# Maxout products of three chunks by Strassen's seven products, all v loads and nearly all stores on SyncE, and a new order table

## The chip, the cores and the metric

The kernel runs on one core of a Trainium2 chip. The metric is the device time of one execution in microseconds (us). The core has five engines that run their own instruction lists and wait for each other through semaphores: TensorE (PE; its weight loads are counted apart as PEld), VectorE (DVE), ScalarE (ACT), GpSimd (POOL) and SyncE (SP, which here only issues DMAs). Matrix products land in PSUM, which has eight banks per partition, each as wide as 512 f32 numbers; DVE or ACT must copy a result out before its bank is free for another product.

## The reference: what is computed

An attention with feature maps (8 batches, 8 heads, 576 tokens, head size 64, 128 features) feeds a maxout layer (4608 tokens, model size 512, inner size 768):

```
def phi(x):
    proj = np.einsum('bhsd,df->bhsf', x, w_phi)
    proj = proj - np.max(np.abs(proj), axis=-1, keepdims=True)
    return np.concatenate([np.exp(proj), np.exp(-proj)], axis=-1)
q_p, k_p = (phi(q), phi(k))
kv = np.einsum('bhsf,bhsd->bhfd', k_p, v)
z = np.sum(k_p, axis=2)
num = np.einsum('bhsf,bhfd->bhsd', q_p, kv)
den = np.einsum('bhsf,bhf->bhs', q_p, z)[..., None] + 1e-06
...
h = np.maximum(np.maximum(x @ w1, x @ w2), x @ w3)
return (h @ w_out).astype(np.float32)
```

Here `x` is the attention's output, with the heads side by side.

## The kernel before

**Attention** is done in 16 units: one batch and four of its eight heads each. A unit loads q and k as bf16 (POOL's DMA queue), v as f32 (`v_raw`, L435), and the last 64 tokens of q (`tail_raw`, L426). It turns q and k so that the head size lies along the partitions (`qkT`): the first four units on PE (L459), the others by transposing DMAs on SP (L478). It projects (`psk`, `psq`, `pst`, L496), takes the largest absolute value of each row on DVE (L500), and exponentials on ACT (`Ek` L504, `Eq` L584). POOL scales v by a factor per token (`vab`, L548), PE multiplies this with `Ek` (`kvps`, L567) and `Eq` with that (`psn`, L632); DVE adds the two halves (L641, L644) and POOL divides (`x_sb`, L690). A transposing DMA on SP (L722; PE in the first two units) puts the result, turned, into `xT`.

Most of the projections and the `kvps` products use 64 of PE's 128 rows at a time (`mode=1` in the code), two of them side by side. The projection of the last tokens (L600) uses all 128 rows, with a weight tile whose upper half is zero (`wph_low`).

**The maxout layer** is done in nine chunks of 512 tokens: chunks 0 to 7 are the first 512 tokens of each batch, chunk 8 is the last 64 tokens of all batches. It uses max(a, b, c) = a + max(0, b − a, c − a): POOL first replaces w2 and w3 by their differences to w1 (L844, six pieces), and since the `a` part goes through `w_out` unchanged, w1 and `w_out` are multiplied once ahead (`pm`, L865) and applied to x directly (`straight`, L781). So a chunk is 2 × 6 products `ups` (L748), each of four 128x512 matmuls; the first kind is copied out with a relu (ACT L762 or DVE L764), the second is maximized into it by DVE (L758) to give `hT`; then four groups of `straight` (four matmuls each, L781) and `down` (six, L786), a copy `osb` (L796) and a store (L800).

**The order** is no loop order: every piece of work is a node, and the table `PLAN` lists all nodes with the engine that runs them, the start for which they were set, and the buffer or PSUM bank that they take. Each engine runs its nodes in the table's order; the starts themselves have no effect on the chip, but for `fill`, which puts idle matmuls (`idler`, L911) into gaps of the first 30 us.

## Time and profile before

| | |
|---|---|
| time, median of 3 runs | 282.42 us (282.17 to 282.78) |
| span of the profiled execution, first to last instruction | 280.8 us |
| own time of the profiled execution | not listed; the median lies 1.6 us above its span |
| PE busy | 268.3 us, 3409 matmuls in the records |
| DVE busy | 217.3 us |
| ACT busy | 199.1 us |
| POOL busy | 161.5 us |
| TensorE clock granted | 1.00 throughout |

A busy share is the time in which an engine has at least one instruction under way. Matmuls overlap: one of 512 columns lasts 379 ns, but the next one starts well before it ends, so the pace of PE is read from the time that a run of equal matmuls takes, not from the mean of one. DVE and ACT instructions overlap a little in the same way.

### The profile page before, as it was taken

The page shows a single profiled execution, that of the slowest core. Times are in us where ns is not written, and L with a number is a line of the kernel's source. Part 1 is how long each engine was busy: PE and PEld are TensorE (multiplying, and loading weights), DVE is VectorE, ACT ScalarE, POOL GpSimd, SP SyncE. Part 2 cuts the span into 40 slices and gives each one's busy share as a digit, 9 for nine tenths or more (in the row PEclk, how much of TensorE's full clock was granted, in tenths as well). Part 3 has the DMA queues.
Part 4 walks back from the last instruction along what each step waited for, and adds up shares of the span by engine and source line. Part 5 has one row for each costly group of instructions (what it writes and reads, how often), then busy time and mean ns, then how long its engine had stood idle before and what let it go on. Part 6 is the DMA issues. An engine that isn't in the chain of part 4 may idle for free. (4 is left out here: it accounts for less than half of the span.)

```text
span 280.8 us, 8401 instructions
## 1 busy us (share of the span) xinstructions
PE 268.3 (96%) x3409; PEld 150.8 (54%) x3447; DVE 217.3 (77%) x442; ACT 199.1 (71%) x489; POOL 161.5 (58%) x161
## 2 busy tenths in 40 slices
PE   8789899999999999999999999999999999999993
PEld 5457654576655555555555456655546544444441
DVE  2799989999999969889997899898876871157320
ACT  4799999999999787698978879989589200310001
POOL 4879999998949703897336848393495341000000
PEclk9999999999999999999999999999999999999999
DMA  7999999997999999999999997717130224110253
GB/s 136 300 202 208 207 173 310 260 164 132 171 186 249 236 196 281 169 171 144 189 263 204 188 276 125 151 55 170 39 86 3 77 47 121 40 75 0 82 144 112
DMA packets 76214, 44.52 MB, mean 159 GB/s; under 512 B 52688, under 2 KB 67344, under 8 KB 76176
## 3 DMA queue, kind: packets, MB, share of 16 engines
q1 hardware_dynamic: 59536, 29.21, 49.8%
q0 software_dynamic: 14912, 11.77, 28.7%
q10 hardware_dynamic: 1728, 3.02, 3.0%
q8 instruction: 27, 0.44, 0.7%
q14 instruction: 11, 0.09, 0.1%
HBM read 34.64 MB, written 9.44 MB: 157 GB/s over the span
## 5 line engine op out<-in xcount | busy, mean ns | idle before, releaser
L748 PE MATMUL ups<-xT,w_bf 128*128 128x512 bf16 x414 | 101.3, 379 | 1.0
L584 ACT ACTIVATE Eq<-psm 128x512 bf16<-128x512 f32 (+1 forms) x160 | 81.7, 587 | 5.4 <-PE psm L593 3.1
L548 POOL TENSOR_TENSOR vab<-v_raw,em 128x1152 bf16<-128x1152 f32 (+1 forms) x36 | 68.2, 1907 | 22.9 <-ACT em L542 15.0
L504 ACT ACTIVATE Ek<-psk 128x512 bf16<-128x512 f32 x128 | 72.1, 633 | 8.2 <-PE psk L496 6.3
L748 PEld LDWEIGHTS <-w_bf 128*128 128x128 bf16 x432 | 39.2, 98 | 43.9 <-issue 2.3
L690 POOL TENSOR_TENSOR x_sb<-y,rden 128x640 bf16<-128x640 f32 x32 | 39.9, 1256 | 39.5 <-DVE rden L689 39.0
L786 PE MATMUL ops<-wout_bf,hT 128*128 128x512 bf16 (+2 forms) x214 | 50.5, 373 | 0.3
L758 DVE TENSOR_TENSOR hT<-hT,ups 128x512 bf16<-128x512 bf16 x54 | 35.5, 677 | 13.3 <-PE ups L748 11.1
L500 DVE TENSOR_REDUCE mq<-psq 128x4 f32<-128x512 f32 x64 | 41.2, 682 | 3.5 <-PE psq L496 3.2
L500 DVE TENSOR_REDUCE mk<-psk 128x4 f32<-128x512 f32 x64 | 41.9, 679 | 2.1 <-PE psk L496 1.7
L762 ACT ACTIVATE hT<-ups 128x512 bf16<-128x512 f32 x36 | 21.9, 620 | 24.5 <-PE ups L748 24.4
L641 DVE TENSOR_TENSOR y<-psn,sq 128x325 f32<-128x325 f32 x64 | 30.4, 491 | 6.7 <-PE psn L632 4.3
L796 ACT COPY osb<-ops 128x512 f32<-128x512 f32 x20 | 12.2, 608 | 32.3 <-PE ops L786 31.8
L786 PEld LDWEIGHTS <-hT 128*128 128x128 bf16 x222 | 20.6, 98 | 22.5 <-issue 0.2
L632 PEld LDWEIGHTS <-Eq 128*128 128x128 bf16 x640 | 26.3, 98 | 10.3 <-issue 0.4
L644 DVE TENSOR_TENSOR y<-y,psn 128x325 f32<-128x325 f32 x64 | 29.7, 487 | 1.6
L632 PE MATMUL psn<-kv_sb,Eq 128*128 128x65 bf16 x640 | 28.8, 194 | 0.2
L496 PEld LDWEIGHTS <-qkT 64*128 64x128 bf16 x576 | 18.0, 94 | 13.4 <-issue 8.3
L781 PE MATMUL ops<-xT 128*128 128x512 bf16 x87 | 23.7, 380 | 0.5
L567 PE MATMUL kvps<-vab,Ek 64*128 64x65 bf16 x1152 | 22.1, 191 | 0.8 <-POOL vab L548 0.6
L567 PEld LDWEIGHTS <-Ek 64*128 64x128 bf16 x1152 | 20.3, 94 | 3.4 <-issue 1.3
L796 DVE COPY osb<-ops 128x512 f32<-128x512 f32 (+2 forms) x17 | 11.1, 657 | 12.5 <-PE ops L786 12.5
(65 smaller groups left out, 263.9 us busy)
## 6 DMA issues: line engine op xcount, KB each, us to landing
v_raw<-in_v_dram SPq DMA_DIRECT2D x15, 576.0 KB, 6.0
out_dram<-osb SPq DMA_DIRECT2D x23, 256.0 KB, 3.3
qk_bf<-in_k_dram POOLq DMA_DIRECT2D x15, 288.0 KB, 6.9
qk_bf<-in_q_dram POOLq DMA_DIRECT2D x15, 256.0 KB, 8.7
w_bf<-in_moe_w_dram POOLq DMA_DIRECT2D x3, 768.0 KB, 13.2
out_dram<-osb ACTq DMA_DIRECT2D x9, 256.0 KB, 3.4
tail_raw<-in_q_dram SPq DMA_DIRECT2D x16, 64.0 KB, 4.8
wout_bf<-in_moe_w_out_dram POOLq DMA_DIRECT2D x1, 768.0 KB, 19.2
```

Of the source, the lines that this page charges most:

```text
L500: return nd(kind, {"DVE": 0.598 if n == 4 else 0.331}, lambda: nc.vector.tensor_reduce(dst(m()), ps()[:, 0:n, :], AXX, ALU.max, apply_abso ...
L504: return nd("ek", {"ACT": 0.478 if n == 4 else 0.264}, lambda: nc.scalar.activation(dst(Ek[g]()), ps()[:, 0:n, :], EXP, scale=1.0 - 2.0 * ...
L548: made.append(chosen(n_, lambda n_, g=g, t0=t0, t1=t1: (nc.vector if n_.eng == "DVE" else nc.gpsimd).tensor_tensor(vab()[:, g, t0:t1, 0:D] ...
L567: nc.tensor.matmul(kvps[ab]()[:, pr, g, :], lhsT=Ek[g]()[r, t, :], rhs=vab()[r, g, t, :], start=(pr == prs[0] and g + j == 0), stop=(pr == ...
L584: return nd("eq", {"ACT": 0.478 if n == 4 else 0.264}, lambda: nc.scalar.activation(Eq[g]()[:, t0:t0 + n, :], ps()[:, 0:n, :], EXP, scale= ...
L632: nc.tensor.matmul(psn[g]()[:, i, :], lhsT=Eq[g]()[:, t, :], rhs=kv()[:, pr, ab, g, :], start=True, stop=True)
L641: n_ = nd("xu", {"DVE": 0.064 + 0.0676 * n_t}, lambda: nc.vector.tensor_tensor(yv(y()), ps(0), sq_of(sq()).unsqueeze(len(shape) - 1).to_br ...
L644: return nd("xw", {"DVE": 0.064 + 0.0674 * n_t}, lambda: nc.vector.tensor_tensor(yv(y()), yv(y()), ps(1), ALU.add), [n_], [psn[1], y], loc ...
L690: divs[pr] = nd("x", {"POOL": 1.2}, lambda pr=pr, y=y, rden=rden: nc.gpsimd.tensor_tensor(x_sb()[:, pr].rearrange("p t a d -> p a t d"), y ...
L748: nc.tensor.matmul(ups()[:, o * n:(o + 1) * n], lhsT=w_bf[i + (not plain)][:, ct, jj * P:(jj + 1) * P], rhs=tokens_of(ct)[:, cols] if halv ...
L758: nc.vector.tensor_tensor(dst, dst, src, ALU.max)
L786: nc.tensor.matmul(ops_()[:, 0:hi - lo], lhsT=hT()[:, j, tt * P:(tt + 1) * P], rhs=wout_bf[:, j, lo:hi], start=plain and j == 0, stop=(j = ...
```

## The change

**Seven products.** In chunks 6, 7 and 8 the two products of x with the weight differences are no longer made one after the other. The tokens of a chunk are cut in two halves and the model size in two halves, so x is a 2 by 2 array of quarters; the two weight differences with their two halves of the model size are another 2 by 2 array. Their product, four results of 256 tokens by 128 inner columns for each of two weight columns, is made from seven quarter products instead of eight (Strassen's scheme in Winograd's form). It goes in three pairs of inner columns per chunk. Per pair:

- PE makes seven products of four 128x256 matmuls (function `product` inside `seven_products`) instead of four products of four 128x512 matmuls.
- ACT copies the first product to SBUF as f32 (`us`).
- DVE makes seven additions of a product in PSUM and an earlier f32 part in SBUF (`uj`, function `joined`); four of these results are the four quarters, of which two are written straight into `hT` and two as bf16 over the place of an older part.
- ACT applies the relu to the two quarters in `hT`, in place (`hr`), and DVE takes the maximum of each with its partner (`hx`, both operands bf16 in SBUF).

Ahead of that come four sums or differences of quarters of x per chunk (`xs`, all on POOL) and, once for all chunks, twelve of the weights (`ws`, ten on POOL, two on DVE). The parts lie in the buffers of `v_raw`, the sums of x in those of `qkT`, the sums of the weights in those of `qk_bf`.

**Queues.** All loads of v go through SP (one went through ACT), all stores too but one (ten went through ACT); the load of `w_phi` moves from ACT to SP.

**The last tokens' projection** (`mm_t`, L600) takes over the row mode of the PE node that stands ahead of it: nine of sixteen now use 64 rows.

**New table.** `PLAN` is new from the first to the last row; its costs for SP's nodes were set anew. `fill` now places idle matmuls with regard to the order in which banks are taken: there are 41 instead of 57.

```
+EITHER = 2
+SEVEN = (6, 7, 8)
...
-9G0@1.2 10S0@0.8 3A@1.1 1D@0.8 2G@1.9 16S0@1.3 0G@2.1 103G1@2.7 104G@7.2 4A@1.8 12D@4.0 8G@7.5 6D@4.2 11A@4.0
...
+    mode = 0
+    for n in order:
+        if n.eng == "PE":
+            if n.mode == EITHER:
+                n.mode = mode
+            mode = n.mode
...
-        main_v = chosen(nd("Lv", {"SP": 0.42, "ACT": 0.6}, None, [], [vraw], xfer=[(16, 93.0, 0.42)]),
+        main_v = chosen(nd("Lv", {"SP": 0.68}, None, [], [vraw], xfer=[(16, 93.0, 0.42)]),
...
+            def product(moving, weight, deps, uses):
+                ps = bank("ups", [P, 2, n])
+
+                def fn():
+                    for o, j in enumerate(js):
+                        for c in range(2):
+                            m = quarter_of(*moving) if isinstance(moving, tuple) else sums()[:, moving]
+                            nc.tensor.matmul(ps()[:, o, :].rearrange("p (b t) -> p b t", t=m.shape[-1]) if len(m.shape) == 4 else ps()[:, o, :],
+                                             lhsT=weight()[:, c, j * P:(j + 1) * P], rhs=m[:, c], start=o + c == 0, stop=o + c == 2)
+                return ps, ff("up", {"PE": 0.435}, fn, deps, [ps] + uses)
...
+            def joined(p, other, dst, tile, then=()):
+                ps, a = p
+                src, used, e = other
+                return ff("uj", {"DVE": 0.598}, lambda: nc.vector.tensor_tensor(runs(dst()) if dst not in own else dst(), runs(ps()), runs(src()), ALU.add),
+                          [a, e] + list(then), [ps, used, tile], locks=[ps])
...
+            p1 = product((0, 0), lambda: w_bf[1][:, 0:2], ready + d2, [])
+            s1 = chosen(ff("us", {"ACT": 0.482, "DVE": 0.598}, None, [p1[1]], [p1[0], one_], locks=[p1[0]]),
+                        lambda n_: copy_on[n_.eng](one()[:, 0], p1[0]()))
...
+            c11 = joined(p2, s1, own[0], hT)
+            p6 = product(1, lambda: w_sums[1](), [made[1], n_w[1][jp]], [sums_, w_tiles[1]])
+            u2 = part(one, 1), one_, joined(p6, s1, part(one, 1), one_)
...
+            for i, (x, y), to in ((0, (c11, c12), first), (1, (c21, c22), second)):
+                r_ = ff("hr", {"ACT": 0.478}, lambda i=i: nc.scalar.activation(h(i)(), h(i)(), RELU), [x], [hT])
+                to.append(chosen(ff("hx", {"DVE": 0.35}, None, [r_, y], [one_, hT], port=True),
+                                 lambda n_, i=i: on[n_.eng].tensor_tensor(h(i)(), h(i)(), runs(low(i)()), ALU.max)))
...
-                    s_ = ff("store", {"SP": 0.41, "ACT": 0.6} if n_out == 1 else {"SP": 1.2}, None, [e], [osb],
+                    s_ = ff("store", {"SP": 0.6} if n_out == 1 else {"SP": 1.2}, None, [e], [osb],
```

How the order stands at three places follows; names are those of the code, an arrow points from what is read to what is written.

On DVE, the end of the list before: L764 is the relu of a first product, L758 the maximum with a second one, L796 the copy of a finished output.

```order
L764 TENSOR_SCALAR hT<-ups 128x512
L796 COPY osb<-ops 128x512
L758 TENSOR_TENSOR hT<-hT,ups 128x512
L764 TENSOR_SCALAR hT<-ups 128x512
L758 TENSOR_TENSOR hT<-hT,ups 128x512 x5
L764 TENSOR_SCALAR hT<-ups 128x512
L758 TENSOR_TENSOR hT<-hT,ups 128x512
L764 TENSOR_SCALAR hT<-ups 128x512
L758 TENSOR_TENSOR hT<-hT,ups 128x512 x4
L796 COPY osb<-ops 128x128
L796 COPY osb<-ops 128x384
L796 COPY osb<-ops 128x512 x4
```

Six copies of outputs, from chunks 7 and 8, close the list. The end of DVE's list in the changed kernel, where L830 are the joins (`uj`), L865 the maxima (`hx`) and L940 the copies of outputs:

```order
L830 TENSOR_TENSOR hT<-ups,parts 128x2x256
L830 TENSOR_TENSOR parts<-ups,parts 128x512
L865 TENSOR_TENSOR hT<-hT,parts 128x2x256
L830 TENSOR_TENSOR parts<-ups,parts 128x512 x3
L865 TENSOR_TENSOR hT<-hT,parts 128x2x256 x2
L830 TENSOR_TENSOR parts<-ups,parts 128x512 x2
L865 TENSOR_TENSOR hT<-hT,parts 128x2x256
L830 TENSOR_TENSOR hT<-ups,parts 128x2x256
L830 TENSOR_TENSOR parts<-ups,parts 128x512
L865 TENSOR_TENSOR hT<-hT,parts 128x2x256
L940 COPY osb<-ops 128x512 x2
L940 COPY osb<-ops 128x128
```

The joins fill DVE's list almost to its end, and its last row is now a copy of 128 columns; in the whole list 63 joins and 18 maxima of SBUF tiles stand in place of 18 maxima and 11 relus of PSUM tiles.

On POOL, in the units 1 to 3 of the start, before: L690 is the division of the first two units, L844 a weight difference, L548 the scaling of v for units 2 and 3.

```order
L690 TENSOR_TENSOR x_sb<-y,rden 128x2x5x64
L430 CAST qk_bf<-tail_raw 128x2x64
L844 TENSOR_TENSOR w_bf<-w_bf 128x4x256
L690 TENSOR_TENSOR x_sb<-y,rden 128x2x5x64
L393 DMA qk_bf<-in_k_dram 128x2x576
L690 TENSOR_TENSOR x_sb<-y,rden 128x2x5x64
L844 TENSOR_TENSOR w_bf<-w_bf 128x4x256 x3
L383 DMA qk_bf<-in_q_dram 128x4x256
L844 TENSOR_TENSOR w_bf<-w_bf 128x4x256
L430 CAST qk_bf<-tail_raw 128x2x64
L548 TENSOR_TENSOR vab<-v_raw,em 128x18x64 x4
```

Divisions and weight differences take turns, and the four scalings follow each other. The same place in the changed kernel, where the lines are L742, L988 and L598:

```order
L742 TENSOR_TENSOR x_sb<-y,rden 128x2x5x64
L443 DMA qk_bf<-in_k_dram 128x2x576
L742 TENSOR_TENSOR x_sb<-y,rden 128x2x5x64 x3
L988 TENSOR_TENSOR w_bf<-w_bf 128x4x256 x6
L598 TENSOR_TENSOR vab<-v_raw,em 128x18x64 x3
L443 DMA qk_bf<-in_k_dram 128x2x576
L433 DMA qk_bf<-in_q_dram 128x4x256
L598 TENSOR_TENSOR vab<-v_raw,em 128x18x64
```

All four divisions now stand ahead of the six weight differences, and two DMA issues ahead of the last scaling.

On ACT, the end of the list before:

```order
L762 ACTIVATE hT<-ups 128x512 x7
L800 DMA out_dram<-osb 128x512
L800 DMA out_dram<-osb 64x128
L796 COPY osb<-ops 128x512 x3
L800 DMA out_dram<-osb 128x512
```

And in the changed kernel (L846 copies a first product, L863 is the relu in place):

```order
L863 ACTIVATE hT<-hT 128x16x32 x2
L846 COPY parts<-ups 128x512
L863 ACTIVATE hT<-hT 128x2x256 x2
L940 COPY osb<-ops 128x512
L863 ACTIVATE hT<-hT 128x2x256 x2
L940 COPY osb<-ops 128x512 x3
L944 DMA out_dram<-osb 64x128
```

Before, the last store of all is issued by ACT for a full 128x512 tile; now ACT's only store is half of the last 128-column piece, and SP issues the others.

More of the change, by code (lines that the diff above doesn't have):

```diff
@@ L202 @@
+1686S@271.3 1687A@271.0
+"""
 ENGINES = {"T": "PE", "D": "DVE", "A": "ACT", "G": "POOL", "S": "SP"}
@@ L255 @@
+    return todo
 @with_exitstack
@@ L295 @@
     copy_on = {"DVE": nc.vector.tensor_copy, "ACT": nc.scalar.copy, "POOL": nc.gpsimd.tensor_copy}
+    on = {"DVE": nc.vector, "POOL": nc.gpsimd}
     queue_of = {"SP": nc.sync, "ACT": nc.scalar, "POOL": nc.gpsimd}
@@ L730, in chunk @@
+    def chunk(c_i, ready, tokens_of, tile_of, out_rows, n_out, quarter_of):
         hT = buf("hT", 2, [P, JT, SM], BF16)
@@ L737, in chunk @@
         halves, plain = len(ready) == 2, c_i < RAW0
-        for half in range(1 + halves):
+        seven = c_i in SEVEN
+        if seven:
+            evac = seven_products(c_i, ready[0], quarter_of, hT, ff)
+        for half in range(0 if seven else 1 + halves):
             for i in range(2 + plain):
```

404 lines of the change are left out of this document (255 added, 149 removed).

## The prediction

> **What bounds the kernel now.** First the head of the page and the busy times by stretch (start:end, length, then busy us and count of each engine, granted clock, DMA share, GB/s).
>
> ```profile
> PE 268.3 (96%) x3409; PEld 150.8 (54%) x3447; DVE 217.3 (77%) x442; ACT 199.1 (71%) x489; POOL 161.5 (58%) x161
> ...
> 0.00:20.00 20.00, 16.30 (x161) 10.29 (x161) 12.64 (x29) 13.96 (x36) 13.66 (x26) 1.00 1.06 213
> 20.00:40.00 20.00, 18.65 (x379) 13.52 (x380) 19.04 (x45) 19.66 (x52) 19.95 (x19) 1.00 1.20 199
> 40.00:60.00 20.00, 19.74 (x312) 11.05 (x315) 19.40 (x38) 19.61 (x54) 19.55 (x17) 1.00 1.12 249
> 60.00:80.00 20.00, 19.71 (x272) 11.46 (x275) 19.04 (x44) 19.50 (x50) 18.52 (x17) 1.00 1.03 160
> ...
> 140.00:160.00 20.00, 19.20 (x230) 10.37 (x233) 17.24 (x34) 17.11 (x42) 11.20 (x12) 1.00 1.19 229
> ...
> 180.00:200.00 20.00, 19.79 (x255) 11.03 (x260) 18.08 (x38) 16.38 (x41) 12.10 (x10) 1.00 0.45 103
> 200.00:220.00 20.00, 19.69 (x306) 11.44 (x309) 15.20 (x31) 15.98 (x41) 12.63 (x14) 1.00 0.16 45
> 220.00:240.00 20.00, 19.89 (x118) 9.57 (x119) 10.60 (x23) 1.64 (x3) 4.97 (x7) 1.00 0.32 86
> 240.00:260.00 20.00, 19.95 (x96) 9.29 (x97) 10.21 (x16) 4.14 (x9) 0.00 (x0) 1.00 0.11 40
> ```
>
> From 40 us on PE is idle for at most 0.3 us in 20 (0.8 in one stretch), at a full clock, so PE's list sets the end. DVE, ACT and POOL are as full as PE from 20 to 60 us, and nearly empty after 220. Then the chain of waits, whose last 120 us are PE, for the real pace of matmuls (start, length, what):
>
> ```profile
> 172.46 0.11 PE psm L600
> ...
> 184.47 0.55 PE psk L496 x16
> ...
> 186.65 2.59 PE ups L748 x12
> ...
> 205.79 0.86 PE ops L781 x4
> ...
> 208.27 0.45 PE psq L496 x16
> 208.72 0.97 PE ops L781 x4
> ...
> 261.53 0.34 PE ops L786 x6
> ...
> 276.24 0.03 ACTq L796
> 276.26 0.04 issue
> 276.30 0.59 ACT osb L796
> ```
>
> A 128x512 matmul costs 2.59/12 = 0.216 us of PE's list, a 128x128 one 0.34/6 = 0.057, each with a weight load of its own. The pairs of equal groups show one thing more: four matmuls take 0.86 us after work on all 128 rows, but 0.97 after `psq`, which uses 64 rows; sixteen `psk` take 0.55 after `ops`, on 128 rows, but sixteen `psq` 0.45 after 64-row work. So each change between 64 and 128 rows costs PE 0.10 us. PE ends at 276.24; 4.5 us of copy and store follow.
>
> **The seven products, −3.6 us.** Out go 3 chunks × 48 matmuls × 0.216 = 31.1 us. In come 3 × 84 = 252 matmuls of 256 columns. The line through 0.057 at 128 and 0.216 at 512 gives 0.110 at 256, and the one 256-column matmul in the chain (L600) shows 0.11; half of 0.216 is the least, 0.108. So 27.2 to 27.7 us, and the saving lies between 3.4 and 3.9; I take 3.6. Weight loads stay hidden, as they do for the 128-column matmuls.
>
> **More row changes, +1.4 us.** Counted along PE's list, 64 and 128 rows change 102 times before and 116 times in the changed kernel, although nine of the sixteen L600 matmuls now take over the mode ahead of them; the new table cuts the projections into smaller groups. 14 × 0.10 = 1.4. The bounds are 0, if the added ones fall where PE waits anyway, and 1.5; they lie mostly between units 4 and 12, where PE doesn't wait, so 1.4.
>
> **The DVE stage at the end, +0.7 us.** The rows for DVE's pace:
>
> ```profile
> 63.90 0.49 DVE L641 TENSOR_TENSOR y<-psn,sq 128x325 f32<-128x325 f32 x1
> 64.30 0.48 DVE L644 TENSOR_TENSOR y<-y,psn 128x325 f32<-128x325 f32 x1
> ...
> 251.68 2.48 DVE L758 TENSOR_TENSOR hT<-hT,ups 128x512 bf16<-128x512 bf16 x4 [1.56 <-ACT hT L762]
> ...
> 261.90 0.29 DVE L796 COPY osb<-ops 128x128 f32<-128x128 f32 x1 [0.74 <-PE ops L786]
> ```
>
> ```profile
> L500 DVE TENSOR_REDUCE mq<-pst 128x2 f32<-128x256 f32 x16 | 6.6, 415 | 2.3 <-PE pst L496 2.3
> L689 DVE RECIPROCAL rden<-y 128x10 f32<-128x10 f32 x32 | 6.4, 206 | 0.2
> L844 POOL TENSOR_TENSOR w_bf<-w_bf 128x1024 bf16<-128x1024 bf16 x6 | 12.6, 2121 | 0.0
> ```
>
> Four L758 in a row take 2.48 us with the last at 0.68, so one costs 0.60 of DVE's list. A join reads PSUM and an f32 tile in SBUF; L644 does the same with 325 elements and takes 0.40 from start to start (0.48 less the overlap of 0.08), also directly after the L641 whose result it needs. By length that is 0.60 for 512, so 63 joins cost 37.8. No row shows a maximum of two bf16 SBUF tiles (`hx`). It costs at least what a 256-element operation does (0.415 − 0.08 = 0.33, if two elements go at a time) and at most 0.60; I take 0.35, nearer to the first: the rows at one element a step all have f32 or PSUM on a side, and this one has neither. 18 × 0.35 = 6.3. With five pairs of L641 and L644 (4.0), four reciprocals (0.5) and two copies (1.1) that stand among them, DVE needs 49.7 us from the first join to the last maximum. PE, from the end of the second product to chunk 7's first `down`, has by its list 61 products (26.6), 14 groups of `straight` (11.9), 10 of `down` (12.6), and 2.0 of attention: 53.1. Less 1.1 for the last relu and maximum, DVE has 2.3 us to spare: the forecast stands on that. Its bounds are 0 and +3.5 (below). The nearest row is 40 to 80 us, where DVE is over 95% busy and PE loses 0.26 + 0.29 us in 40; over 53 us that is 0.7.
>
> The Trainium skill, "VectorE: DVE Perf Modes", section "The perf-mode tier table (the rule you actually need)", has a `tensor_tensor` of bf16 in SBUF go at twice the rate of f32 (1224 against 2293 ns for 2048 elements), and one with a PSUM operand at the single rate. By the page `hx` costs the lower bound and the spare time is 2.7 us; by L758's row, taken for all, it would be 2.2 us short. No run here shows `hx` yet.
>
> **The start, +0.5 us.** POOL is 19.95 and 19.55 of 20 us busy between 20 and 60, so its list paces that stretch. In the changed list one more DMA issue stands ahead of the last scaling (L548) of unit 3, and PE's `kvps` of that unit wait for it; that row and PE's longest waits before:
>
> ```profile
> L393 POOL DMA_DIRECT2D qk_bf<-in_k_dram x15 | 11.0, 733 | 0.0
> ...
> PE tps L459 <- DMA qk_bf<-in_k_dram: 1.6, 1, 1.6
> ...
> PE kvps L567 <- POOL vab L548: 0.6, 1, 0.6
> ```
>
> One issue is 0.7 us. The new order of the first loads (k of unit 1 now stands first in POOL's queue, `w_phi` second in SP's) can take the 1.6 us wait away or bring one like it. Bounds: −2.2 if both waits vanish, +2.2 if they come twice. I take +0.5.
>
> **What costs nothing.** The sums `xs` and `ws` on POOL are 22 × 1.06 us (half of L844's 2.12) = 23 us; POOL has 7 to 8 us free in every 20 from 180 on, and 15 from 220. Without that cover, chunk 6's products would wait, 1 us per sum. ACT's 18 relus and 9 copies, at most 0.6 each, fall after 210 us, where it works 1.6 and 4.1 us in 20. SP gets eleven more issues; in the rows below a store from SP lands as soon as one from ACT, and behind a store that waits for its `osb` stand transposes and v loads. PE would see that as waits of `psk` and `kvps`; I take 0, since its waits on DMA after 40 us are none now.
>
> **The end, −0.4 us.** Last now is a 128-column piece on DVE (0.29 us, above) with 32 KB stores; before, ACT's 0.59 us and a full tile:
>
> ```profile
> out_dram<-osb SPq DMA_DIRECT2D x23, 256.0 KB, 3.3
> ...
> out_dram<-osb ACTq DMA_DIRECT2D x9, 256.0 KB, 3.4
> ...
> out_dram<-osb ACTq DMA_DIRECT2D x1, 32.0 KB, 2.1
> ```
>
> But the last full tile ends only ten 128-column matmuls earlier (0.57 us) and still lands 3.3 us after its issue. So the gain is at most 0.6, at least 0; I take 0.4.
>
> **Sum.** −3.6 + 1.4 + 0.7 + 0.5 − 0.4 = −1.4: a span of 279.4 in place of 280.8. The median of the runs lies 1.6 above the span of before; with the same distance, 281.0 us against 282.42. A difference under 0.2% (0.56 us) can't be told from none here.
>
> **Rivals.**
>
> 1. *Nothing new waits.* DVE and the start keep up: −3.6 + 1.4 − 0.4 = −2.6, 279.8 us. For it: PE lost nothing to DVE after 220 us, and its banks let it run ahead. Against it: DVE goes from 10 to about 19 us of 20 there.
> 2. *DVE becomes the bound of the last 55 us.* The place is the joins of chunks 6 to 8; the price is `hx` at 0.60 and joins at 0.62: DVE's 49.7 grows by 18 × 0.25 + 63 × 0.02 to 55.5, that is 3.5 over what PE leaves it. −3.6 + 1.4 + 0.5 + 3.5 − 0.4 = +1.4: 283.8 us, slower. It decides from a DVE sum of 54.7 on, where the loss passes 2.7. For it: no row has an all-SBUF bf16 operation, and ends must follow a chain of seven joins. Against it: the joins' form is L644's, which overlaps.
> 3. *The start loses a second set of waits*, +2.2 in place of +0.5: 282.7 us, no change. For it: the first loads are in a new order, and POOL, DVE and ACT are all full from 20 to 60. Against it: the work is the same.
> 4. *DVE and POOL block each other.* `hx` has two SBUF inputs, which no DVE operation of before has, while POOL makes the `xs` of chunks 7 and 8. If each waits for the other's instruction, four maxima of chunk 6 wait up to 1.06 us, half of that on average: 2.1 us of DVE's list, 2.3 of which it has to spare, so about +1.0 beyond the forecast: 282.0 us. The Trainium skill, "SBUF — State Buffer", section "SBUF: two separate sides", states such an exclusive lock for a DVE operation with two SBUF inputs against a GpSimd one. No run here shows it yet.
> 5. That the change doesn't do what it says is no rival: the lists hold 252 matmuls of 256 columns for 144 of 512.
>
> **How the numbers follow.** Forecast 0.45; rival 1 0.15; rival 2 0.15; rival 3 0.17; rival 4 0.08. Faster: of the forecast 0.38 (its terms can miss by 0.8), rival 1 all, 0.03 each of rivals 3 and 4: 0.59. Slower: 0.12 of rival 2, 0.04 of 3, 0.01 each of 4 and the forecast: 0.18. The rest, 0.23, is no change. The range goes from 279.0, rival 1 with some of the start's waits gone, to 283.2, short of rival 2's full price: 279.0 to 283.2.
>
> **What would show it.** Right: 252 `ups` matmuls with runs at 0.108 to 0.110; joins 0.60 and `hx` 0.33 to 0.36 apart; PE over 19.6 of 20 us busy after 220 with no wait on DVE; `kvps` of unit 3 up to 0.7 later; the last copy 0.3 us. Wrong: PE waits on DVE in the last 55 us (rival 2), on DMA or `vab` before 60 us (rival 3), DVE gaps that a POOL instruction ends (rival 4); or PE's row changes cost nothing, which would give 1.4 back.

## The result, and the profile after

The changed kernel takes 290.09 us, median of four runs (288.33 to 291.97), against 282.3 us for the kernel before on the same chip: a ratio of 1.0275, 95% interval 1.0228 to 1.0322. It is slower by 7.8 us; the forecast was 281.0. Here and below a median holds all timed runs, and a ratio leaves out the slow ones, which took over 1.5% longer than the fastest run of the same kernel. In the profiled execution the span is 288.4 us in place of 280.8.

The head of the page of the changed kernel, and its busy times by stretch (columns as before: stretch, length, then busy us and count for PE, PEld, DVE, ACT and POOL, granted clock, DMA share, GB/s):

```profile
PE 268.3 (93%) x3500; PEld 160.4 (56%) x3539; DVE 250.7 (87%) x494; ACT 213.5 (74%) x513; POOL 186.6 (65%) x181
...
0.00:20.00 20.00, 15.24 (x155) 9.48 (x157) 13.06 (x28) 13.43 (x30) 12.99 (x24) 0.85 1.05 195
...
80.00:100.00 20.00, 19.69 (x301) 10.83 (x299) 18.12 (x38) 19.11 (x44) 11.69 (x11) 1.00 1.15 204
100.00:120.00 20.00, 16.88 (x221) 9.22 (x220) 14.39 (x29) 13.23 (x36) 13.73 (x15) 1.00 1.08 193
...
160.00:180.00 20.00, 17.99 (x223) 9.61 (x226) 19.34 (x34) 16.49 (x44) 12.65 (x11) 1.00 0.61 137
...
200.00:220.00 20.00, 18.48 (x292) 10.63 (x289) 18.00 (x34) 15.88 (x40) 15.98 (x14) 1.00 0.50 112
220.00:240.00 20.00, 19.31 (x230) 14.23 (x227) 19.24 (x42) 9.96 (x23) 17.75 (x19) 1.00 0.24 62
240.00:260.00 20.00, 19.16 (x137) 13.05 (x138) 19.63 (x32) 7.64 (x15) 7.42 (x6) 1.00 0.04 14
260.00:280.00 20.00, 19.84 (x125) 12.31 (x127) 18.44 (x35) 6.68 (x12) 0.00 (x0) 1.00 0.30 89
```

Before, PE lost nothing worth naming after 40 us. Now three stretches stand out, with 16.88, 17.99 and 18.48 us in place of 19.2 to 19.8, and two smaller ones from 220 to 260. None of the first three was a term of the forecast. PE's three longest waits in them, from the timeline of the changed kernel (start, length, what, and in brackets the idle time just before and what ended it):

```profile
107.47 0.40 PE L546 MATMUL psk<-wph,qkT 64*128 64x128 bf16 x8 [2.79 <-DMA qkT<-qk_bf]
...
178.04 0.38 PE L546 MATMUL psk<-wph,qkT 64*128 64x128 bf16 x7 [1.63 <-DVE hT L902]
...
209.81 0.44 PE L684 MATMUL psn<-kv_sb,Eq 128*128 128x65 bf16 x9 [1.21 <-DVE hT L902]
```

**An account of PE's time.** PE's list can be priced by itself: each matmul at the pace of its form (0.216 us for 512 columns, 0.109 for 256, 0.056 for 128, and so on) and 0.096 per change between 64 and 128 rows. Whatever the start of a matmul lies later than that sum is time in which PE had nothing to do. The points are the first `kvps` of some units (counted from 0) and PE's last matmul; "mended" is the experiment with both mends, below.

| PE without work, us | before | changed | mended |
|---|---|---|---|
| start to the second `kvps` of unit 1 | 9.85 | 12.80 | 12.6 |
| to unit 6 | 3.2 | 3.5 | 3.7 |
| unit 6 to unit 7 | 0.2 | **3.4** | 0.2 |
| unit 7 to unit 11 | 1.4 | 0.6 | 0.6 |
| unit 11 to the end | 0.3 | **7.3** | 3.6 |
| sum | 14.9 | 27.6 | 20.8 |
| PE's list itself | 260.9 | 256.4 | 256.4 |

PE's last matmul starts at 275.84 before, and at 284.04 now: 4.5 us less list, 12.7 us more waiting. The list is shorter by 3.6 for the products and by 1.7 for 16 idle matmuls fewer, longer by 1.3 for the row changes; the other 0.5 are L651 matmuls that use half the array. So the saving is there. The question is where 12.7 us of waiting come from.

**First, from SyncE's queue.** Its issues in the changed kernel (start, length, what):

```profile
79.15 1.74 SPq L944 DMA_DIRECT2D out_dram<-osb  x1
87.08 2.23 SPq L774 DMA_TRANSPOSE xT<-x_sb  x1
89.37 3.29 SPq L485 DMA_DIRECT2D v_raw<-in_v_dram  x2
92.76 4.32 SPq L528 DMA_TRANSPOSE qkT<-qk_bf  x2
...
99.17 2.24 SPq L774 DMA_TRANSPOSE xT<-x_sb  x1
101.52 1.35 SPq L528 DMA_TRANSPOSE qkT<-qk_bf  x1
```

SyncE stands still from 80.9 to 87.1, at the head of its queue the transfer of unit 4's x, whose `x_sb` isn't ready (SyncE's wait for POOL's division is 6.1 us). Behind it stand the v loads of units 8 and 7 and both transfers of unit 9, then x of unit 5, and last k of unit 8. All come out as one burst, each issue 0.6 to 3.0 us (some rows above hold two), and PE needs first what comes last: k of unit 8, issued at 101.52, lands at 107.4, and PE has waited for it since 104.7. Of the transfers ahead of it, q of unit 9 is used some 18 us after it by the table's own times (119.0 and 100.6).

**Second, from DVE's new operations.** Two of the twelve weight differences (`ws`, L1002) stand on DVE. The timelines of DVE and of POOL around the first:

```profile
173.87 3.44 DVE L1002 TENSOR_TENSOR w_sums<-w_bf,w_sums 128x512 bf16<-128x512 bf16 x1
177.24 0.20 DVE L741 RECIPROCAL rden<-y 128x10 f32<-128x10 f32 x1
```

```profile
173.76 0.77 POOL L443 DMA_DIRECT2D qk_bf<-in_k_dram  x1
174.53 1.05 POOL L1030 COPY w_bf<-xT 128x1024 bf16<-128x1024 bf16 x1
175.51 0.30 POOL L480 CAST qk_bf<-tail_raw 128x128 bf16<-128x128 f32 x1
175.77 1.25 POOL L742 TENSOR_TENSOR x_sb<-y,rden 128x640 bf16<-128x640 f32 x1
177.52 1.26 POOL L742 TENSOR_TENSOR x_sb<-y,rden 128x640 bf16<-128x640 f32 x1 [0.50 <-DVE rden L741]
```

DVE starts its sum 0.11 us after POOL has begun, and ends it 0.29 us after POOL's fourth instruction, in the first gap that POOL leaves. The second took 2.00 us at 207.15 and ended 0.27 us after one POOL operation of 2.12. The maxima of the first chunk of seven products do the same, beside POOL's `xs`; a row of the tile's view, and rows of DVE's timeline at 239 and 245 us (POOL busy) and at 262 (POOL empty):

```profile
L865 DVE TENSOR_TENSOR hT<-hT,parts x18: 412/418/1371, 235.4 to 279.3; 128x512 bf16<-128x512 bf16 x18
```

```profile
239.04 2.51 DVE L865 TENSOR_TENSOR hT<-hT,parts 128x512 bf16<-128x512 bf16 x2
...
244.58 1.90 DVE L865 TENSOR_TENSOR hT<-hT,parts 128x512 bf16<-128x512 bf16 x2
...
262.31 0.75 DVE L865 TENSOR_TENSOR hT<-hT,parts 128x512 bf16<-128x512 bf16 x2
```

Two maxima take 0.75 us where POOL is empty, 1.90 and 2.51 where it isn't. So far this is only a coincidence in time; whether POOL is the cause is tested below.

### The profile page after: what moved, and what is told of

Its sections match the earlier page's. It is cut to its first block, busy times and chain, and to the rows that moved or that the text cites. A ratio compares the mean times of both kernels' runs of the same rounds, so it can differ in the third digit from the quotient of the medians.

```text
span 288.4 us, 8720 instructions
## 1 busy us (share of the span) xinstructions
PE 268.3 (93%) x3500; PEld 160.4 (56%) x3539; DVE 250.7 (87%) x494; ACT 213.5 (74%) x513; POOL 186.6 (65%) x181
## 4 chain that ended last, share of the span: by engine, by line
PE 71%; DVE 10%; ACT 6%; issue 5%; DMA 5%; POOL 2%; DVEq 0%; POOLq 0%; ACTq 0%
PE ups L892 16%; PE ops L930 14%; PE ops L925 10%; PE ups L821 7%; PE psn L684 6%; PE kvps L617 6%; PE psq L546 3%; ACT Eq L634 3%; DMA qk_bf<-in_q_dram 2%; PE psm L643 2%; PE psk L546 2%; DMA qkT<-qk_bf 2%; DVE w_sums L1002 2%; PE pm L1024 1%; DVE mq L550 1%
## 5 line engine op out<-in xcount | busy, mean ns | idle before, releaser
L598 POOL TENSOR_TENSOR vab<-v_raw,em 128x1152 bf16<-128x1152 f32 (+1 forms) x36 | 68.3, 1908 | 21.0 <-ACT em L592 20.9
L554 ACT ACTIVATE Ek<-psk 128x512 bf16<-128x512 f32 x128 | 73.0, 636 | 10.2 <-PE psk L546 7.3
L892 PE MATMUL ups<-xT,w_bf 128*128 128x512 bf16 x273 | 68.2, 379 | 1.2 <-DMA xT<-x_sb 0.2
L930 PE MATMUL ops<-wout_bf,hT 128*128 128x512 bf16 (+2 forms) x217 | 51.7, 373 | 0.4
L742 POOL TENSOR_TENSOR x_sb<-y,rden 128x640 bf16<-128x640 f32 x32 | 40.0, 1255 | 16.9 <-DVE rden L741 16.7
L892 PEld LDWEIGHTS <-w_bf 128*128 128x128 bf16 x288 | 25.6, 97 | 27.9 <-issue 2.3
L684 PEld LDWEIGHTS <-Eq 128*128 128x128 bf16 x640 | 25.4, 97 | 10.6 <-issue 2.8
L830 DVE TENSOR_TENSOR parts<-ups,parts 128x512 f32<-128x512 f32 (+1 forms) x45 | 29.2, 681 | 1.3 <-PE ups L821 0.8
L863 ACT ACTIVATE hT<-hT 128x512 bf16<-128x512 bf16 x18 | 11.0, 631 | 25.2 <-DVE hT L830 25.1
L902 DVE TENSOR_TENSOR hT<-hT,ups 128x512 bf16<-128x512 bf16 x36 | 24.0, 675 | 2.6 <-PE ups L892 1.6
L617 PEld LDWEIGHTS <-Ek 64*128 64x128 bf16 x1152 | 21.2, 95 | 3.5 <-issue 1.3
L940 ACT COPY osb<-ops 128x512 f32<-128x512 f32 x26 | 15.5, 600 | 9.8 <-PE ops L930 9.7
```

The source lines that it names most:

```text
L554: return nd("ek", {"ACT": 0.478 if n == 4 else 0.264}, lambda: nc.scalar.activation(dst(Ek[g]()), ps()[:, 0:n, :], EXP, scale=1.0 - 2.0 * ...
L598: made.append(chosen(n_, lambda n_, g=g, t0=t0, t1=t1: (nc.vector if n_.eng == "DVE" else nc.gpsimd).tensor_tensor(vab()[:, g, t0:t1, 0:D] ...
L617: nc.tensor.matmul(kvps[ab]()[:, pr, g, :], lhsT=Ek[g]()[r, t, :], rhs=vab()[r, g, t, :], start=(pr == prs[0] and g + j == 0), stop=(pr == ...
L684: nc.tensor.matmul(psn[g]()[:, i, :], lhsT=Eq[g]()[:, t, :], rhs=kv()[:, pr, ab, g, :], start=True, stop=True)
L742: divs[pr] = nd("x", {"POOL": 1.2}, lambda pr=pr, y=y, rden=rden: nc.gpsimd.tensor_tensor(x_sb()[:, pr].rearrange("p t a d -> p a t d"), y ...
L892: nc.tensor.matmul(ups()[:, o * n:(o + 1) * n], lhsT=w_bf[i + (not plain)][:, ct, jj * P:(jj + 1) * P], rhs=tokens_of(ct)[:, cols] if halv ...
```

## The experiments

In the variants of the changed kernel the order table is wrapped otherwise, so their line numbers are 29 lower than the changed kernel's: `hx` is L836 (L865 there), `ws` L973, `xs` L771, `ups` of the seven products L792. Times are those of the timed runs; the account of PE's waiting is from the one profiled execution of each.

### The two `ws` on POOL

```diff
-1177D1@166.8 ... 1185D@197.7
+1177G1@166.8 ... 1185G@197.7
```

> The changed kernel, but the two weight differences (`ws`, L1002) that stood on DVE are computed by POOL; nothing else moves. Lock theory (a DVE operation with two SBUF inputs cannot run while POOL runs, and gets its turn only in a gap of POOL): the two stalls of DVE, 3.4 us at 174 and 2.0 us at 207, vanish, and with them PE's waits behind `hT` of 1.6 and 1.2 us and what follows from them. Time 286 to 287.2 us, that is 3 to 4 us under the changed kernel's 290.1. Rival, DVE is simply too full for its new work: DVE loses two operations of 0.42 us, so at most 0.8 us comes back, 289.3 us or more.

Measured: 286.14 us, runs from 283.2 to 290.2, ratio 1.0116 (1.0048 to 1.0183). The median is 3.9 us under the changed kernel's, and the interval lies apart from its 1.0228 to 1.0322. PE's waits of 1.6 and 1.2 us are gone; between 170 and 214 us PE waits 0.3 us in place of 4.0. Two operations of 0.42 us, moved off DVE, gave 3.7 us of PE's time between unit 11 and the end. DVE's fullness can't explain that: it would give 0.8. In this execution PE also had no wait for k of unit 8, with the old list of SyncE; the section on the list by need comes back to that.

### One transfer earlier in SyncE's list

```diff
 401S@83.5 ...
+615S1@94.2        # k of unit 8
 614S0@85.0        # v of unit 8
 544S3@85.7 685S0@86.4 684S@87.9 1235S@90.7 751S1@91.2 470S@92.7
-615S1@94.2
```

> The changed kernel, but in SyncE's list one transposing transfer (k of unit 8, to qkT) is issued one place earlier, ahead of the second v load of unit 8, whose own issue took 2.66 us. Queue theory (PE's 2.8 us wait of `psk` at 104.5 comes from SyncE's issues of 2 to 3 us each standing one behind the other): the transfer is issued 2 to 3 us earlier and the wait shrinks to under 0.5 us; time 287 to 288 us, and K of unit 7 starts 2 to 3 us earlier against the changed kernel's 112.1. Rival (the transfer itself is slow, since the DMA rings are busy): the wait stays above 2 us and the time at 290.

Measured: 290.10 us, ratio 1.0168 (1.0098 to 1.0238). The runs are spread: 285.4 and 287.8 lie below every run of the changed kernel, 292.4 and 294.3 above every one. In the profiled execution, one of the long ones, k of unit 8 was issued at 89.56 and was in time. But now x of unit 5 was late:

```profile
105.86 0.58 PE L863 MATMUL ups<-xT,w_bf 128*128 128x512 bf16 x1 [3.85 <-DMA xT<-x_sb]
```

So in this execution both theories missed: the wait neither went nor stayed, it moved to the next transfer of the same burst. What happened in the two short runs isn't shown, since no trace of them was kept. The next idea was that the whole of what stands behind SyncE's stop at 81 us counts.

### `xs` of chunks 7 and 8 on DVE

```diff
-1606G0 1608G 1607G 1521G2 1522G 1609G 1524G 1523G
+1606D0 1608D 1607D 1521D2 1522D 1609D 1524D 1523D
```

> The changed kernel, but the eight `xs` of chunks 7 and 8 run on DVE and not on POOL, so that POOL has nothing left to do while DVE makes the maxima `hx` of chunk 6. Lock theory: all `hx` take 0.41 to 0.43 us as they do after 250 us now (four of chunk 6 took 0.60 to 1.37), PE loses 1.5 to 2.5 us less between 220 and 250 us, and DVE's eight more operations of 0.35 us (2.8 us) cost at most 1 us of that again: 288 to 289.5 us. Rival 2 of the prediction (DVE itself is the bound of the last 55 us): 2.8 us more on DVE make it slower by 1 to 2.8 us, 291 to 293 us.

Measured: 289.38 us, ratio 1.0256 (1.0198 to 1.0314): not to be told from the changed kernel. The first half of the expectation came as written: all 18 maxima now take 0.42 us. The second didn't. PE now waits for a sum that stands in DVE's list behind five joins and two maxima:

```profile
239.71 0.61 PE L792 MATMUL ups<-sums,w_sums 128*128 128x256 bf16 x4 [1.75 <-DVE sums L771]
```

That the maxima wait for POOL is shown; that this costs PE anything by itself isn't. The later runs come back to it.

### More idle matmuls at the start

```diff
-                if t + d > n.start - 0.12:
+                if t + d > n.start - 0.12 + (0.55 if n.kind == "T" and 5.0 < n.start < 15.5 else 0.0):
```

> The changed kernel with 13 more idle matmuls (54 for 41) in the first 15 us, ahead of the transposes that PE waited for at 5.6, 8.7 and 11.1 us. If the drop of the granted clock to 0.5 between 14.4 and 21.6 us came from the idle stretches before it, the clock stays at 1.00 there, and the first `kvps` starts up to 1.5 us earlier. How much of it reaches the end: the lag of PE behind its own table grew by only 0.3 us from the kernel before to the changed one up to unit 6, so I expect 289 to 290, 0 to 1 us under the changed kernel. Rival (the start is what costs most): 286 to 287 us.

Measured: 290.52 us, ratio 1.0277. The clock held, as the first stretch of the changed kernel (0.85 above) and of this one shows:

```profile
0.00:20.00 20.00, 15.59 (x196) 10.45 (x196) 13.87 (x31) 14.26 (x34) 12.91 (x25) 1.00 1.06 195
```

Nothing came of it: the second `kvps` of unit 1 starts at 30.30 us, between the 30.04 and 31.17 us of the four other executions with this order. PE waits for first loads there, at any clock. In this execution, too, PE waited 2.2 us for k of unit 8 at 103 us.

### SyncE's list by need

```diff
-401S 614S0 544S3 685S0 684S 1235S 751S1 470S 615S1 1275S
+544S3 401S 615S1 1235S 751S1 470S 684S0 614S0 685S 1275S
```

> The changed kernel with another order in SyncE's list alone, by who needs what first: v of unit 7, x of unit 4, k of unit 8, x of unit 5, and only then k of unit 9, v of unit 8 and q of unit 9 (before: x of unit 4, for which SyncE waits from 81 to 87 us, and behind it both v loads and both transfers of unit 9, then x of unit 5 and k of unit 8). Queue theory in its second form (what stands behind the wait at 81 us comes out as one burst in which every transfer lands 4 to 7 us after its issue, and those that PE needs first stand last in it): no wait of PE on a transfer between 95 and 112 us in any run, `kvps` of unit 7 at 108 to 109 us in place of 112.1, a time of 286 to 287.2 us with a spread between runs under 1.5 us (the earlier experiment on one transfer ranged from 285.4 to 294.3). Rival (the transfers are slow whatever their order): waits of 2 to 4 us stay, and the time stays at 288 to 292.

Measured: 288.47 us, ratio 1.0225 (1.0184 to 1.0267), runs from 287.2 to 289.5. SyncE's issues, and PE's first use of k of unit 8:

```profile
81.73 0.89 SPq L456 DMA_DIRECT2D v_raw<-in_v_dram  x1
89.12 1.61 SPq L745 DMA_TRANSPOSE xT<-x_sb  x1
90.84 3.39 SPq L499 DMA_TRANSPOSE qkT<-qk_bf  x1
...
98.01 1.36 SPq L745 DMA_TRANSPOSE xT<-x_sb  x1
```

```profile
106.31 0.40 PE L517 MATMUL psk<-wph,qkT 64*128 64x128 bf16 x8
```

SyncE still stops, now until 89.1, and the row of `psk` has no wait. The time fell by less than expected, and the two intervals overlap, so the time alone shows nothing. In the profiled execution the start took 2 us longer than in the others (PE without work for 14.9 us by unit 1), which hides part of the gain there; why the other three runs gained no more isn't shown. The traces say more: of the five executions above (the changed kernel's and the first four experiments') three show a wait of 2.2 to 3.9 us between units 6 and 7, two show none; of the seven with the new list (this run and the six below) none does. The old order cost something in some executions, not in all.

### Both mends

The last list and the two `ws` on POOL, together.

> The order by need in SyncE's list, and the two `ws` on POOL in place of DVE. If the two causes add: PE's idle time grows by 3.2 and 3.9 us less than in the changed kernel, so the time is 290.1 - 7.1 = 283.0 us, with 282.5 to 284 for every run; still 0.5 to 1.5 us slower than the kernel before, since the start, the row changes and the maxima of chunk 6 are as in the changed kernel. Rival (what is freed early waits later at the same place): 285 or more.

Measured: 283.15 us, ratio 1.0031 (1.0005 to 1.0057). Expected were 283.0. Eleven of twelve runs lie between 281.3 and 284.7. Together the two causes are 7 us of the 7.8. The account above shows that they add: unit 6 to 7 falls from 3.4 to 0.2, and unit 11 to the end from 7.3 to 3.6. (The medians of the runs with one mend each, 1.6 and 3.9 us under the changed kernel, add to 5.5 only.) What stays is the start and 2.3 us of PE's time between 221 and 242 us. The new list may have a price of its own, by v of unit 8, which is loaded later now: in five of the seven executions with it PE waits 0.4 to 1.2 us for `vab` at 125 us; in this one it doesn't.

### The maxima as copies

```diff
-on[n_.eng].tensor_tensor(h(i)(), h(i)(), runs(low(i)()), ALU.max)
+on[n_.eng].tensor_copy(h(i)(), runs(low(i)()))
```

> As the run with both, but each `hx` is a copy of the second half (one SBUF input) and no maximum of two: this leaves the maximum over the second relu's half out, and is for its time alone. Lock theory (only an operation with two SBUF inputs waits for POOL): the six operations of chunk 6 take as long beside POOL's `xs` as those of chunks 7 and 8 without POOL, and PE's idle time between 225 and 245 us falls by 2 us or more: 280.5 to 281.5 us. Rival (DVE is too full there, lock or not): PE's waits stay and the time falls by less than 0.7 us.

Measured: 282.42 us, ratio 1.0014 (0.9979 to 1.0049), 0.7 us under both mends. The experiment missed its aim, since four of the six copies of chunk 6, 0.28 us alone, took 0.95, 1.23, 0.48 and 1.24 us beside POOL. An operation with one SBUF input waits as well. The theory that only two inputs make the lock fell here, and the next two runs look for the rule. The run says one thing about DVE's time, too: the six copies took 4.4 us in all, for 6.0 of the maxima with both mends, and from the first `kvps` of unit 15 PE needed 63.6 us to its last matmul, for 65.0. Most of that gain stands before 247 us.

### The lock by itself

Two runs of the kernel before with operations added behind its last output; the core of the first, and the kinds of the second:

```diff
+    two(4)                                            # maxima of two bf16 tiles, alone
+    for i in range(14):
+        nc.gpsimd.tensor_tensor(a[:, 1 + i % 2, 0:SM], a[:, 3, 0:SM], a[:, 3, 0:SM], ALU.subtract)
+    for i in range(4):
+        nc.vector.tensor_copy(b[:, i % 2, 0:SM], b[:, 2, 0:SM])
+    for i in range(4):
+        nc.vector.tensor_tensor(f[:, 0:SM], ps, f[:, 0:SM], ALU.add)
+    two(4)
...
+        nc.vector.tensor_tensor(f[:, 0:SM], g[:, 0:SM], g[:, SM:2 * SM], ALU.add)        # f32 and f32
+        nc.vector.tensor_tensor(b[:, i % 2, 0:SM], b[:, 2, 0:SM], g[:, 0:SM], ALU.max)   # bf16 and f32
+        nc.vector.tensor_tensor(b[:, i % 2, 0:SM], ps, b[:, 2, 0:SM], ALU.max)           # PSUM and bf16
```

> The kernel before with a measurement behind its last output (its own time means nothing): DVE runs four maxima of two bf16 tiles (128x512) alone, then four copies, four additions of PSUM and SBUF and four maxima while POOL runs fourteen subtractions back to back, then four maxima beside ten POOL multiplications of f32 tiles (128x640), then four beside fourteen POOL copies. Lock theory: alone 0.41 to 0.43 us; copies and additions beside POOL as without it (additions 0.60 apart); each maximum beside POOL's operations with two inputs 1.0 us or more, as one POOL operation at least has to end first; beside POOL's copies, with one input, I expect less, and don't know. Rival (the stalls of the changed kernel come from late inputs, not from POOL): all maxima 0.41 to 0.43 us.

> The kernel before with a second measurement behind its last output (its own time means nothing): which DVE operations wait for POOL. Alone and beside back-to-back POOL subtractions: a sum of two f32 tiles in SBUF, a maximum of a bf16 and an f32 tile in SBUF, a copy f32 to f32, a maximum of PSUM and bf16; then maxima of two bf16 tiles beside POOL's mixture of a DMA issue, a copy, a cast and a multiplication. If two SBUF inputs are what locks, both sums with two SBUF inputs wait (1.0 us or more), the f32 copy too only if it runs two elements a step (0.3 us alone for 512), and PSUM and bf16 stay at 0.69. If only two elements a step lock (the bf16 maximum and the bf16 copy of the first measurement), the f32 forms run at their lone pace. Beside the mixture a maximum that is passed over by several POOL instructions takes 2 us or more, as the `ws` did in the changed kernel (3.4).

DVE's timeline in the first run, beside POOL's subtractions (copies, additions with PSUM, maxima), and at last beside POOL's copies:

```profile
278.28 3.42 DVE L941 COPY w_bf<-w_bf 128x512 bf16<-128x512 bf16 x4
281.61 2.85 DVE L943 TENSOR_TENSOR probe_f<-probe_ps,probe_f 128x512 f32<-128x512 f32 x4
284.38 4.01 DVE L927 TENSOR_TENSOR w_bf<-w_bf 128x512 bf16<-128x512 bf16 x4
...
306.88 3.14 DVE L927 TENSOR_TENSOR w_bf<-w_bf 128x512 bf16<-128x512 bf16 x4
```

And in the second, first alone, then beside POOL's subtractions (from 284 us on):

```profile
277.37 1.42 DVE L935 TENSOR_TENSOR probe_f<-probe_g 128x512 f32<-128x512 f32 x2
278.82 0.89 DVE L937 COPY probe_f<-probe_g 128x512 f32<-128x512 f32 x2
279.62 1.29 DVE L939 TENSOR_TENSOR w_bf<-w_bf,probe_g 128x512 bf16<-128x512 bf16 x2
282.02 0.75 DVE L927 TENSOR_TENSOR w_bf<-w_bf 128x512 bf16<-128x512 bf16 x2
...
284.66 2.47 DVE L949 TENSOR_TENSOR w_bf<-probe_ps,w_bf 128x512 bf16<-128x512 f32 x4
287.05 5.54 DVE L951 TENSOR_TENSOR probe_f<-probe_g 128x512 f32<-128x512 f32 x4
292.51 5.86 DVE L953 TENSOR_TENSOR w_bf<-w_bf,probe_g 128x512 bf16<-128x512 bf16 x4
298.29 4.79 DVE L955 COPY probe_f<-probe_g 128x512 f32<-128x512 f32 x4
```

Per operation, from start to start, alone and beside POOL's subtractions: PSUM and bf16, 0.60 and 0.60; two bf16 tiles, 0.335 and 1.18; bf16 and f32, 0.60 and 1.45; two f32 tiles, 0.72 and 1.45; a copy f32 to f32, 0.46 and 1.18. (The additions of the first run write the tile that the next one reads, and step by 0.73.) All five forms tried that read only SBUF wait, with one or two inputs, bf16 or f32; the maximum of PSUM and bf16 doesn't. Beside POOL's subtractions the two engines take turns, one instruction each, and POOL loses, too: its subtraction goes from a step of 1.00 to 1.18 to 1.45 us. Beside POOL's copies a maximum costs 0.75. Beside the mixture of a DMA issue, copy, cast and multiplication, two of six maxima took 1.83 and 1.62 us: each waited for the POOL instruction under way (a cast, a DMA issue) and then for one more (the multiplication, the copy). In the changed kernel the first `ws` waited for a DMA issue and for three instructions more; why the turns are not kept there, these runs don't show.

The Trainium skill, "SBUF — State Buffer", section "SBUF: two separate sides", says that DVE and GpSimd share a pair of ports as an exclusive lock, held for a whole instruction, and names DVE operations in a two-port mode or with two SBUF inputs. The trace agrees with it on two SBUF inputs (1.18 and 1.45 us for 0.335 and 0.72) and on the maximum with an input in PSUM, which kept its 0.60. The copies waited as well (1.18 us for 0.46); that they run in a two-port mode no run shows.

### All row changes

```diff
             if n.mode == EITHER:
-                n.mode = mode
+                n.mode = 0
```

> The run with both mends (order by need, `ws` on POOL), but the L651 matmuls take no mode over: all sixteen use 128 rows, which raises the changes between 64 and 128 rows in PE's list from 116 to 124. If a change costs PE 0.096 us wherever PE doesn't wait, 8 more cost 0.8 us: 283.9 us, and PE's own list is 0.8 to 1.2 us longer at the same idle time. Rival (the changes hide in waits): 283.1 as with both mends.

Measured: 284.08 us, ratio 1.0041 (1.0009 to 1.0073), 0.9 us over both mends, as expected, but the intervals overlap widely. In the profiled execution the list is longer by the expected sum, yet from unit 3's `kvps` on PE ends only 0.3 us later than with both mends: the rest fell into waits. So a row change is 0.096 us of PE's list. How much of it reaches the end these runs don't say.

### The second halves in f32

```diff
             def low(i):
+                if c_i == 6:
+                    return lambda: one()[:, i]
                 return lambda: one()[:, 0, i, :].bitcast(BF16).rearrange("p (o t) -> p o t", o=2)
```

> The run with both mends, but the second halves of chunk 6 stay f32 (they lie in place of partial sums that are used up), so its six `hx` read a bf16 and an f32 tile, and cost 0.60 in place of 0.335 us of DVE when alone: 1.6 us more. If such an operation doesn't wait for POOL, the stalls of 3.5 us go, DVE gains 1.9 us between 227 and 240 us and PE 1 to 1.5: 281.7 to 282.2. If it waits too: 1.2 to 1.8 us each, and 284 or more.

Measured: 285.11 us, ratio 1.0092 (1.0058 to 1.0126), slower than both mends: the six maxima took 1.33, 0.68, 1.17, 1.63, 0.88 and 1.64 us. A maximum of bf16 and f32 waits too, as the second measurement says. But the run is a good gauge for what DVE's time is worth there: its six maxima take 7.3 us in all, for 6.0 with both mends, and PE has 4.3 us without work from 221 us on, for 2.5: 1.3 us more of DVE's list cost PE 1.8 (from the first `kvps` of unit 15 to PE's last matmul 66.5 us, for 65.0).

### The sums on DVE, by need

The eight `xs` on DVE again, upon both mends, placed between the joins by the order in which PE uses them; the second run sets the last of them six joins earlier.

```diff
-1483D 1502D 1474D 1479D 1498D 1476D 1495D 1485D 1504D ... 1605G 1606G0 1608G 1607G 1521G2 1522G
+1483D 1502D 1605G 1606D0 1608D 1474D 1479D 1607D 1498D 1476D 1495D 1485D 1504D 1521D2 1522D (1523D in the second)
```

> The run with both mends, and the eight `xs` of chunks 7 and 8 on DVE, this time set into DVE's list by the order in which PE needs them (the first run with `xs` on DVE had left them behind joins, and PE waited 1.7 us for one). POOL then has nothing to do from about 232 us on. Lock theory: the five slow maxima of chunk 6 (1.07, 1.2, 1.37, 0.6 and 1.37 us) all but the first go to 0.42, so DVE gives back 2.9 us and takes 2.7 for the sums, POOL's 1.2 to 1.3 us per sum is no longer between a landed transfer and PE, and PE's waits of 0.67 at 234 and of some 1.5 us between 235 and 242 shrink: 282.0 to 282.9 us. Rival (the maxima were never what PE waited for; DVE's fullness is): 283.1 or more.

> As the run before, but the last of the eight sums stands six joins earlier in DVE's list; it was what PE waited 1.06 us for at 243 us. If the maxima of chunk 6 were a cost of their own, PE keeps the 1.1 us that it was ahead at 242 us of the run with both mends, and ends there: 282.1 us, 1 us under it. Rival (DVE's list is the bound of this stretch, and the wait only moves): PE waits as long at the next join, and the time stays at 283.1 to 283.8.

Measured: 283.75 us, ratio 1.0054 (1.0021 to 1.0088), and 283.85 us, ratio 1.0047 (1.0021 to 1.0074): neither can be told from 283.15. In the first, the maxima take 0.41 us but for the first, PE is 1.1 us ahead at 242 us, and loses it at the last sum:

```profile
PE ups L792 <- DVE sums L771: 1.1, 1, 1.1
```

In the second that wait is gone, and PE's time without work from 221 us on is 2.05 us, for 2.47 with both mends. The stretch from 222 to 245 us of the changed kernel, of both mends, and of this last run:

```profile
222.00:245.00 23.00, 22.55 (x203) 15.73 (x203) 22.90 (x46) 10.40 (x19) 21.21 (x22) 1.00 0.21 52
```

```profile
222.00:245.00 23.00, 21.59 (x143) 13.41 (x143) 22.90 (x37) 6.93 (x13) 17.17 (x16) 1.00 0.24 63
```

```profile
222.00:245.00 23.00, 21.90 (x145) 14.16 (x146) 22.86 (x46) 7.12 (x13) 7.50 (x8) 1.00 0.24 63
```

DVE is busy for 22.9 of 23 us in all three, with POOL nearly as full or mostly empty. With the maxima at full pace DVE has the sums instead (eight at 0.335 are 2.7 us, about what the waits had cost), and is as full as before. A run with the maxima at full pace and without the sums on DVE was not made; the nearest is the one with copies, in which PE gained 1.4 us. No version found here is faster than the kernel before.

## Why the prediction was wrong

**The seven products, −3.6: right.** 252 matmuls of 256 columns step by 0.109 us (forecast 0.108 to 0.110).

**More row changes, +1.4: right as a price, unclear as a loss.** PE's list grew by 14 × 0.096. The run with eight more couldn't show how much of it reaches the end. The Trainium skill, "TensorEngine Tiling (Array Packing)", section "Key Properties", says that a change of the tiling mode drains TensorE; it gives no time, and 0.096 us is what it takes here.

**The start, +0.5: near as a number, and by luck.** PE's time without work up to unit 1, with 16 idle matmuls fewer allowed for (1.7 us), grew by 1.2 in the profiled execution, and by 0.1 to 1.0 in most of the others; one took 3.3. The forecast put its 0.7 us at unit 3's `kvps`, behind one more DMA issue on POOL; no wait for `vab` stands there in the changed kernel. The growth stands before unit 1's second `kvps`, where PE waits, among smaller waits, 1.0 us for a k and 0.9 for a q (before, 1.6 for a k and none for a q). That is one of the two things the forecast weighed, with bounds of −2.2 and +2.2, so 0.5 was a choice and not a result. The drop of the clock cost nothing that could be measured.

**"What costs nothing": the step that failed first.** It took 0 for SyncE's eleven more issues, "since its waits on DMA after 40 us are none now". That there was no wait before was read as room. It was the result of an order in which nothing that PE needed soon stood behind a long stop. Costing the issues wasn't enough either: the loss isn't in their 0.6 us but in what is queued behind the one that waits, which the forecast named for stores and not for x of unit 4. Price: 3.2 us in the profiled execution, 0 to 6.4 in the others with the old list or with one transfer moved.

**Rival 4, DVE and POOL: the right mechanism, seen at one of its two places.** It was given 0.08 and 282.0 us. It counted only `hx`, and took half of one POOL operation for each. The 22 sums that the prediction counts on POOL leave two `ws` out, and no term of it has them: they stand on DVE, in the middle of the kernel, where POOL works back to back, and there a sum of 0.42 us took 3.44. The two cost 3.7 us. Four `hx` of chunk 6 took 1.22, 1.37, 0.60 and 1.37 us, 2.9 us more than alone, for the 2.1 that rival 4 reckoned.

**The DVE stage at the end, +0.7: the third term that failed.** Joins step by 0.60 and maxima, where POOL is empty, by 0.335, as taken. PE lost 1.8 to 2.5 us there in place of 0.7. Two steps failed, and the runs don't part them. One is the sum over 53 us: 49.7 us of work in them leaves 2.3 to spare on average, but DVE is busy for 22.9 of 23 us from 222 to 245, and has room only later (18.4 of 20 from 260 on). The other is that the maxima of chunk 6 wait for POOL, 2.9 us by the rows, which alone is more than the 2.3; the term has none of it, it stood in rival 4 only. What the runs do show is that DVE's time counts there nearly one for one: with 1.6 us less of it in the six operations of chunk 6 PE gained 1.4, with 1.3 more it lost 1.5 to 1.8. It was rival 2's place, but the joins cost what the forecast took.

**The end, −0.4: right.** From PE's last start to the end of the span it is 4.35 us in place of 4.94.

Sum over the steps, changed against before: −3.6 (products), +1.3 (row changes), −0.5 (L651 on half the array), +1.2 (start), +0.3 (units 1 to 6), +3.2 (SyncE's queue), −0.8 (units 7 to 11), +3.7 (`ws` on DVE), +3.3 (the rest behind unit 11, of which 1.8 from 229 us on), −0.6 (end). That is 7.5 of the span's 7.6.

## What to carry to other kernels

When an edit puts an operation on DVE that reads only SBUF, look at what POOL does in the same microseconds: here such operations waited for the POOL instruction under way, and some for one to three more (0.42 us became 3.44); an operation with one input in PSUM kept its pace. When a queue gets more work, don't count its issues: find the one that waits longest, list what stands behind it, and ask which of these an engine needs first. And spread a stage's work over its own stretches before you call a surplus of 4% room.

## What the runs showed of the hardware that was not expected

A copy on DVE waits for POOL just as an operation with two inputs does: 0.28 us alone and 1.12 beside POOL's subtractions in bf16, 0.43 and 1.14 in f32. A DVE operation that waits can be passed over by the next instructions of POOL, by one in the measurement (1.62 and 1.83 us) and by three in the changed kernel (3.44).

A long stop of PE can cost more than its own time. In the profiled execution with one transfer earlier PE had no matmul for 3.85 us, and the granted clock of the next two stretches of 4 us was 0.53 and 0.62:

```profile
104.00:108.00 4.00, 2.14 (x6) 0.69 (x5) 0.00 (x0) 0.80 (x3) 2.65 (x6) 0.53 1.14 198
108.00:112.00 4.00, 3.78 (x36) 2.07 (x36) 2.86 (x6) 2.69 (x6) 0.05 (x1) 0.62 1.23 248
```

That wait and the low clock together put PE 6.4 us behind the executions with the new list between units 6 and 7. In the changed kernel the stop of 2.79 us left the clock at 1.00. The Trainium skill, "TensorE: Matmul & The Clock Gate", section "What's actually happening", has the clock halved after an idle window of about 3.4 us; the two stops, one on either side of it, agree.

The length of a stop isn't all, though. At the start of the changed kernel no stop of PE between two matmuls was longer than 1.04 us, and yet the granted clock fell (columns: stretch, length, PE's busy us and count, clock, DMA share, GB/s):

```profile
14.00:16.00 2.00, 1.92 (x21) 0.55 1.37 201
16.00:18.00 2.00, 1.95 (x16) 0.50 1.26 192
```

What lowers it there, these runs don't show.
